# A written order for every instruction, eleven matmuls on a constant tile, and a band drained by head halves

## The chip, the cores and the metric

The kernel runs on one core of a Trainium2 chip. The metric is the device time in microseconds of one execution; the median of the runs shown is compared. The engines are TensorE (PE; PEld are its weight loads), VectorE (DVE), ScalarE (ACT), GpSimd (POOL) and SyncE (SP). POOL and SP only start DMAs here, apart from one mask that POOL makes.

## The reference

Inputs: x of 8 batches x 4224 tokens x 192 channels, a convolution weight of 8 heads x 7 taps, and three matrices w_q, w_k (192 x 64) and w_out (192 x 192), all float32.

```
w   = softmax(weight, over the 7 taps)
y   = causal convolution of x along the tokens: each head of 24 channels with its 7 taps
W   = (y @ w_q) @ (y @ w_k).T / 8          (4224 x 4224 for each batch)
out = relu(W @ y) @ w_out
```

## The kernel before

The 4224 x 4224 matrix is never built: W @ y is (y @ w_q) @ M with M = w_k.T (y.T y) / 8, so a batch needs its Gram matrix y.T y (192 x 192) once. All matrix work is in bfloat16.

*Opening.* `load_w` (SP) brings the taps. POOL makes the identity `ident`; VectorE spreads it to `step`, and TensorE transposes that (`turned`), which ScalarE copies out (`stept`). VectorE also makes `by_tap`, `other` and `own` from the identity, and then the softmax as a chain `mx`, `sub`, `mine`, `ex` (ScalarE), `sm`, `rc`, `wn`, `taps`. From `taps` and `stept` TensorE builds the convolution's band matrix (8 heads, 128 x 128 each): two `fill` products `spread` it to PSUM, half of the columns of all heads in each, and two `band` copies (L527) drain them to the tile BAND, one on ScalarE, one on VectorE. Zeroing of half a dozen tiles lies on VectorE in between.

*A batch.* Tokens are cut into 35 chunks of 122. x is loaded by POOL's queue and cast on the way, in groups of chunks (four groups in batch 0, of 9, 9, 9 and 8 chunks; two in the others). For every group and every pair of heads (`hp` 0 to 3) `gen_conv` multiplies BAND with the chunks; the result is evacuated to `y` (L671). Then follow transposes of y (`tr_lo` L395 and L396, `tr_hi` L726) with evacuations `ytl` and `yth`; the product with w_q (`wq`, L751 and L755) in five token blocks of at most 1024; the Gram matrix (`gram`, L787, six products of up to 6 chunks), its copy (`g`), a transpose (`turn`, `gt`), and the mixing matrix M (`m`, line 829 on) with its copies `ms`. After that, for each token block, `mix_lo` (L878) and `mix_hi` (L890), relu evacuations `rt` and `rh` (L907 ScalarE, L908 VectorE), `fin_hi` (L935) and `fin_lo` with w_out, output copies `out` (L970) and stores by SP (L978). Most products are two halves of 64 columns next to each other in the array ("128x64", recorded at L391 and L392 where the helper `halves` makes them); `mix_lo` and `fin_hi` use halves of 64 rows ("64x128").

*Weights.* SP loads w_q, w_k, w_out (`load_q`, `load_k`, `load_o`, three DMAs each) once the second group of x has landed. ScalarE casts them (L596): three casts `casts_q` that `wq` needs, five `casts_k` that `m` needs, two `casts_o` that `fin_hi` and `fin_lo` need.

*Order.* All work is a list of operations (`Op`), 987 in before. An operation names what it `needs` (waited for by semaphores), what it comes `after` (order alone) and what PSUM banks it takes; seven banks go round, bank 7 holds the Gram matrix. `Planner.plan` walks through time with estimated lengths and gives each operation a place, an engine (evacuations may run on ScalarE or VectorE) and a bank, always the ready operation with the lowest number from the table TURNS. `Program.place` then sets the waits. Each engine runs its own list in that order.

Of the kernel before, what the change touches and what calls it, by code (L numbers as in the profile page):

```python
# [1 line left out]

# [10 lines left out]
TURNS = [  # L13
    int(t) / 1000
    for t in """
-9360 -9860 -8870 -8880 -9260 -9760 -9760 -9160 -9060 -8960 -8910 -8910 -8860 -9360 -9310 -9360 -9360
-9300 -9290 -9280 -8360 -8260 -8210 -8360 -8160 -7960 -7910 -7860 -7360 -7260 -6960 -7260 -4360 -10360
-4260 -4160 -4060 -4040 -3360 -3260 -3160 -4360 -4360 -4360 -4360 -4360 -4360 -4360 -4360 -4360 -4360
-3360 -3340 -3260 -3240 -2360 -2340 -2260 -2240 -1360 -1340 -1260 -1240 -360 -340 -260 -240 640 660 740
760 1640 1660 1740 1760 2640 2660 2740 2760 -480 -5256 -3269 -5639 -2436 -6119 -4785 -6922 -2697 -6547  # L20
-2900 -8184 -3709 -11773 -2741 -3270 -6090 -11945 -3405 -6849 535 -5290 -3070 -5355 -2914 -5199 -4248
-3270 -5203 -8176 -5200 -3617 1049 7270 -1527 1452 -125 437 -1115 2575 669 4462 -4008 2241 -736 2188
-3392 2688 -366 4671 2314 4774 1510 -5859 -1080 1650 3655 -2805 -2225 2863 3712 -4982 -214 3624 -440
5811 168 -43 -4182 2328 1099 2977 4333 5544 2125 -4960 -5487 -5264 -3044 -1246 -5292 -632 -6217 -764
-74 -1078 1645 -1059 -604 310 -1847 1633 809 1261 1148 1774 613 1995 -221 2133 3240 -1868 3227 -220 725
-412 3895 1345 -3908 -437 2412 1145 -3912 1759 7529 -2401 -2511 -376 -45 -770 179 75 1157 1606 377 1178
2478 1419 2696 -2691 660 4785 4565 7183 -1945 323 1366 4118 -874 -955 202 -527 -342 -901 930 -907 356
2535 1985 1382 772 4127 1260 -1111 124 1160 1068 -949 2843 737 1947 1165 1141 1963 1865 1015 1391 1447
1702 -74 1049 2157 -573 -696 2171 3091 -3875 1621 1815 2057 1336 1560 3406 350 3930 1811 1631 806 1533
-2176 120 -160 307 697 392 -607 2158 1443 1095 4683 784 2578 2771 4703 2742 7357 3260 5899 3463 6217  # L30
3645 8560 -333 6048 2165 -3227 -299 4804 1442 -269 2464 1033 2330 -2282 2380 4417 716 -49 3007 5023
2635 1331 4441 4948 2995 6849 3538 5333 2785 2768 -3179 -2909 4430 6167 8185 2441 2170 3478 2909 2541
554 -2341 2444 1927 -821 1930 2471 1683 3865 3015 2812 1681 1913 2901 2236 -1040 2160 2775 2437 2022
2264 1982 2456 530 2945 -625 83 2391 2437 -247 4869 10274 3843 686 -2295 3278 468 -2877 2621 3234 3552
5619 5142 2314 3447 -712 2811 2566 3158 2537 2842 2785 -1373 2551 2194 3151 4852 2972 5013 3067 6779
3044 1235 3763 8267 3776 5123 4769 7025 4778 6514 4876 4862 2843 3189 4464 -186 3400 3287 1517 170 3082
4632 173 2822 4141 2345 4919 -1156 3870 4328 3579 2730 2456 3119 1411 4084 5177 4842 -327 4148 4784
2483 12403 11388 12726 1688 187 6372 10131 3246 4258 -1702 3458 4182 -118 2930 2729 1882 4669 8253 3861
3544 1615 3872 -172 2986 3160 3716 -1740 4531 9062 4005 3598 4951 3990 4363 2435 3391 -188 774 5121
6256 1049 3585 3961 4077 3890 4171 3621 2923 4666 7097 2748 2343 3820 2734 3811 2033 5780 3818 8021  # L40
2648 2954 4015 5571 3280 -1286 3326 1296 4205 -77 4486 1455 4875 3311 5075 4171 5445 4695 5467 3840
5547 6065 4545 4764 3889 874 4988 5384 3296 1407 5065 3706 4229 1167 4799 5495 -1008 2735 5015 4824
-216 1086 4797 3220 6247 4075 6903 8096 2585 2446 2397 3366 12419 11466 9645 4504 4002 2353 3004 4592
2447 1923 4855 3304 3544 3930 4268 4563 -31 1642 3776 4290 -862 3100 4826 6478 4160 4860 2445 3040 6705
3413 4148 6792 4180 4104 2785 4391 4686 4414 786 5937 2381 5714 4010 4678 4791 3602 4621 5486 -3702
4694 4691 4776 4745 8565 4811 2733 1579 4439 3726 3846 1552 3006 3416 5091 3731 3114 391 4950 -191 4947
1241 5561 6938 5922 7844 6076 5816 6857 5549 6431 8495 5919 4361 1180 965 5336 3713 5074 2853 2377 5685
3499 1703 6336 5580 6743 3976 5914 890 3735 -850 6119 5447 4947 4119 5702 6592 2952 2914 3851 5062
11027 10134 10283 4336 4832 2354 5585 5204 5235 5902 4279 5332 6811 4930 5452 70 7184 7777 5311 5310
3592 2752 3699 4914 5160 5093 886 6992 7265 5826 4610 2412 5386 6402 2677 5391 5863 3510 6078 4797 3048  # L50
3549 7308 4286 5112 2810 5621 5940 3872 3652 3847 6176 6516 2312 5811 4551 3444 5310 2800 3910 6703
2902 3118 6150 4601 5838 5604 6069 7926 5802 5058 6795 5408 6694 6497 7055 7466 7544 6117 8040 8562
2857 4878 6430 1709 6339 6247 4084 2149 3587 4651 7375 5911 5923 8233 4224 5104 7135 8548 7626 1422
6752 7520 5954 8811 9981 10001 3331 2861 1100 5523 5736 7942 8989 6855 6991 3418 3771 5267 6754 6792
5257 8583 2774 5930 5621 6098 8589 5981 7588 10163 5667 7262 8790 2009 6160 6573 7890 9275 9286 4367
8366 1994 4430 8376 2928 6391 6798 7671 9079 8471 6945 8447 929 3104 8245 1738 6621 7113 7765 8298
10610 7609 8976 2499 6811 5339 3124 4383 3701 4861 7650 5674 5118 6955 3022 7026 1967 7057 1554 7391
6867 7378 5794 8478 7540 10493 11198 10567 7886 9868 8667 7608 6132 7813 12143 8053 10500 4734 5726
10278 10809 6108 7660 6892 9279 8811 10480 9400 11789 6610 6051 11636 12987 12320 10573 10429 10064
11172 6766 7180 6653 8881 8940 8302 8163 3734 5115 8337 5917 10881 1732 6196 10991 548 6570 3947 6628  # L60
5684 11786 5374 8456 5972 5205 7358 2365 6800 7531 8553 12143 9541 7507 4239 2615 6653 8229 3661 7031
8556 8852 7269 9218 4711 5758 2449 5650 7927 7690 7261 10545 9140 8476 10487 4525 3241 2208 7451 8457
7788 6544 11624 6678 6638 3216 7890 3616 6282 3822 7930 5698 8782 6900 4062 5129 6641 6131 8120 8832
8094 4423 8160 8786 8210 8027 5877 5536 6062 1738 8351 8563 8713 4799 8391 5602 10941 9278 9705 9844
6685 7724 8581 9175 4769 3738 8621 7276 9572 10940 8347 11120 8993 5619 8811
""".split()
]

COL2, ROW2 = "128x64", "64x128"


class Op:


    n = 0

    def __init__(self, engines, emit, ns, needs=(), after=(), banks=0, drains=None, vt=0.0, mode=COL2, tail=0.0):
# [21 lines left out]
        self.size = 0  # L99
        Op.n += 1  # L100
        self.id = Op.n


class Planner:

    LAT = {"PE": 240.0, "ACT": 145.0, "DVE": 140.0, "POOL": 150.0, "SP": 0.0}
    SWITCH = 145.0

    STAY = 0.865

    HOLD = 1

    def __init__(self, nbank, first_bank):
# [164 lines left out]
def bass_lightweight_conv__then__hypermixer_token_mlp_kernel(  # L280
# [93 lines left out]
    def bank(i, n=1):  # L374
        return PS[:, i * 512 : (i + n) * 512]
# [683 lines left out]
```

## Time and profile before

| | us |
|---|---|
| median of 3 runs | 177.33 (177.2 to 178.14) |
| span of the profiled execution, first to last instruction | 175.7 |
| TensorE busy | 157.1 (89% of the span) |
| VectorE, ScalarE, GpSimd busy | 118.0, 123.5, 30.3 |
| all DMA | 40.36 MB, mean 230 GB/s |

The profile is one execution; beside its span it has no time of its own, so the span is held against the median of the runs. Busy shares are averages over stages, and a busy TensorE is not TensorE at its peak: the lengths of its matmuls overlap, so the step from one start to the next is the better measure. "issue" after an idle time means that nothing the profile shows was waited for. A line such as L391 is that of a helper, and stands for several products.

### The profile page before, as it was taken

Reading aid. Unit: us, or ns where it says so; the run is one execution under the profiler, and the core shown is the slowest. Engines: PE = TensorE matmul, PEld = TensorE weight load, DVE = VectorE, ACT = ScalarE, POOL = GpSimd, SP = SyncE. Lnnn points to the kernel's source line nnn. Section 1 sums busy time; section 2 is a strip of 40 time slices with the busy share of each in tenths; the row PEclk is TensorE's granted clock in tenths of the full one; section 3 lists DMA queues with packets and bytes.
Section 4 is the critical chain, followed back from the end, with each engine's and each line's share of the span. In section 5 each row is a group of like instructions: output and inputs, shape, how many; then the busy total and the mean of one; then the engine's idle time right before and its main releaser. Section 6 shows DMA issues by size and latency. Waiting matters only on the chain.

```text
span 175.7 us, 7099 instructions
## 1 busy us (share of the span) xinstructions
PE 157.1 (89%) x3226; PEld 121.7 (69%) x3226; DVE 118.0 (67%) x216; ACT 123.5 (70%) x206; POOL 30.3 (17%) x39
## 2 busy tenths in 40 slices
PE   0289799888999999899989979999999999999990
PEld 0179666776787787668778766878767777877550
DVE  6556587765766677586787738689688675765740
ACT  3243677597787948668648747888888896698980
POOL 7999452524230000000000000000000000000000
PEclk9999999999999999999999999999999999999995
DMA  3999999999999999999999999067283045987787
GB/s 30 162 189 186 205 191 193 191 196 277 193 279 194 286 309 268 343 250 243 304 264 282 237 194 348 24 244 297 103 343 127 4 175 216 356 347 309 265 303 262
DMA packets 48157, 40.36 MB, mean 230 GB/s; under 512 B 37632, under 2 KB 40960, under 8 KB 48128
## 3 DMA queue, kind: packets, MB, share of 16 engines
q0 software_dynamic: 36128, 13.61, 65.1%
q1 hardware_dynamic: 12000, 26.31, 40.9%
q8 instruction: 25, 0.41, 0.9%
q14 instruction: 4, 0.03, 0.1%
HBM read 27.56 MB, written 25.95 MB: 305 GB/s over the span
## 4 chain that ended last, share of the span: by engine, by line
PE 88%; issue 4%; DVE 3%; ACT 2%
PE ps L391 25%; PE ps L787 14%; PE ps L935 8%; PE ps L392 7%; PE ps L395 6%; PE ps L726 6%; PE ps L878 5%; PE ps L751 4%; PE ps L890 4%; PE ps L755 4%; PE ps L396 3%; ACT rt L907 1%; ACT out_sb L970 1%; DVE band L527 0%; DVE xw L416 0%
## 5 line engine op out<-in xcount | busy, mean ns | idle before, releaser
L970 ACT COPY out_sb<-ps 128x768 f32<-128x768 f32 (+1 forms) x46 | 34.7, 768 | 15.1 <-PE ps L392 11.3
L671 ACT CAST y<-ps 122x816 bf16<-122x816 f32 (+3 forms) x46 | 35.7, 791 | 13.2 <-PE ps L392 12.8
L907 ACT ACTIVATE rt<-ps 128x1024 bf16<-128x1024 f32 (+3 forms) x44 | 34.1, 800 | 6.4 <-PE ps L878 4.5
L787 PE MATMUL ps<-y 122*64 122x192 bf16 (+4 forms) x840 | 33.8, 222 | 2.2 <-issue 2.2
L970 DVE COPY out_sb<-ps 128x768 f32<-128x768 f32 (+1 forms) x26 | 21.6, 840 | 19.7 <-PE ps L392 18.5
L392 PE MATMUL ps<-wol,rt 128*64 128x192 bf16 x264 | 33.9, 255 | 1.0 <-issue 1.0
L787 PEld LDWEIGHTS ps<-y 122*64 122x64 bf16 (+1 forms) x840 | 31.1, 112 | 4.9 <-issue 2.8
L565 POOL DMA_DIRECT2D xw<-in_x_dram x34 | 29.9, 893 | 22.3 <-issue 21.5
L391 PE MATMUL ps<-wol,rt 128*64 128x192 bf16 x264 | 33.7, 255 | 0.0
L391 PE MATMUL ps<-xw,band 128*64 128x432 bf16 (+3 forms) x144 | 31.8, 335 | 1.5 <-DVE band L527 0.9
L392 PE MATMUL ps<-xw,band 128*64 128x432 bf16 (+3 forms) x144 | 32.1, 337 | 1.1 <-issue 1.1
L391 PEld LDWEIGHTS ps<-wol,rt 128*64 128x64 bf16 x264 | 24.1, 138 | 8.1 <-issue 2.0
L908 DVE TENSOR_SCALAR rt<-ps 128x512 bf16<-128x512 f32 (+3 forms) x36 | 23.6, 674 | 8.2 <-PE ps L878 7.6
L671 DVE CAST y<-ps 122x864 bf16<-122x864 f32 (+3 forms) x26 | 23.6, 912 | 8.0 <-PE ps L392 7.5
L698 DVE COPY ytl<-ps 128x976 bf16<-128x976 bf16 (+1 forms) x40 | 23.0, 591 | 3.9 <-PE ps L396 3.3
L392 PEld LDWEIGHTS ps<-wol,rt 128*64 128x64 bf16 x264 | 24.1, 138 | 1.2 <-issue 1.2
L396 PE MATMUL ps<-ident,y 122*64 122x122 bf16 x280 | 21.1, 219 | 0.0
L395 PE MATMUL ps<-ident,y 122*64 122x122 bf16 x280 | 21.0, 219 | 0.0
L935 PE MATMUL ps<-woh,rt 64*128 64x192 bf16 x264 | 20.4, 250 | 0.2 <-ACT rt L907 0.2
L395 PEld LDWEIGHTS ps<-ident,y 122*64 122x64 bf16 x280 | 18.1, 112 | 2.0 <-issue 0.5
L726 PE MATMUL ps<-ident,y 122*64 122x122 bf16 (+1 forms) x344 | 17.1, 220 | 1.3 <-DVE y L671 0.7
L396 PEld LDWEIGHTS ps<-ident,y 122*64 122x64 bf16 x280 | 17.7, 112 | 0.0
(95 smaller groups left out, 218.8 us busy)
## 6 DMA issues: line engine op xcount, KB each, us to landing
out_dram<-out_sb SPq DMA_DIRECT2D x28, 768.0 KB, 5.1
xw<-in_x_dram POOLq DMA_DIRECT2D x7, 816.0 KB, 33.2
xw<-in_x_dram POOLq DMA_DIRECT2D x7, 768.0 KB, 33.7
out_dram<-out_sb SPq DMA_DIRECT2D x8, 384.0 KB, 3.3
xw<-in_x_dram POOLq DMA_DIRECT2D x2, 432.0 KB, 8.3
out_dram<-out_sb SPq DMA_DIRECT2D x8, 96.0 KB, 4.3
xw<-in_x_dram POOLq DMA_DIRECT2D x1, 384.0 KB, 5.2
xw<-in_x_dram POOLq DMA_DIRECT2D x8, 45.8 KB, 25.0
```

The lines of the kernel that those rows point to most:

```text
L391: e.matmul(out[0:64], lhsT[:, 0:64], rhs, **k)
L392: return e.matmul(out[64:128], lhsT[:, 64:128], rhs, **k)
L395: e.transpose(out[0:64], in_[:, 0:64], identity)
L396: return e.transpose(out[64:128], in_[:, 64:128], identity)
L565: lambda e, op, part=part: e.dma_start(*part),
L671: return e.copy(dst, src) if op.engine == "ACT" else e.tensor_copy(dst, src)
L726: last = e.transpose(ps[64 * i : 64 * i + HI, o : o + w], Y[0:w, yb, c, LO:D], IDENT[0:w, 0:w])
L787: mm = e.matmul(bank(GB)[p : p + 64, o : o + z - r], Y[0:w, yb, c, r : r + 64], Y[0:w, yb, c, r:z], start=st, stop=end, skip_group_check=True,
L907: return e.activation(dst, src(), AF.Relu)
L908: return e.tensor_scalar(dst, src(), 0.0, None, op0=ALU.max)
L935: last = e.matmul(bank(op.bank + a)[:, o : o + D], RT[64 * a : 64 * a + HI, slot, 2, i:n:nt], WOH[64 * a : 64 * a + HI, :], start=i == q, ...
L970: return e.copy(dst, src) if op.engine == "ACT" else e.tensor_copy(dst, src)
```

## The change

The table TURNS and the planner's search go. In their place stands PLAN, a list of 993 turns, each an operation's number, its engine (P TensorE, A ScalarE, D VectorE, G POOL, S SP) and, for a product, its PSUM bank. `plan` now reads that list. Numbers count the operations as they are added. Those that the prediction speaks of: 0 load_w, 1 the new memset, 15 step, 16, 18 and 37 the three run-ups, 17 turned, 20 by_tap, 22 own, 23 mx, 30 taps, 31 and 34 the fills, 32, 33, 35 and 36 the bands, 38 to 43 the loads of batch 0, 44, 45 and 46 load_q, load_k and load_o, 47 to 49 casts_q, 50 to 54 casts_k, 55 and 56 casts_o, 110 and 112 evacuations y of the last group of batch 0, 143 tr_hi, 151 and 152 grams, 145, 129 and 133 wq, 154 turn, 166 and 160 the first convolutions of batch 1, 881 the last batch's m. POOL's turns are in the same order as before; SP's are not (load_k now stands ahead of load_q, and some stores change places).

Three new TensorE operations multiply a tile RUNUP of zeros with itself, 128 columns by 512, into bank 7: four matmuls ahead of `turned`, six between it and the fills, one between the fills and the first convolution.

The band: a fill now makes all columns of four heads (16 pairs of halves in all, of 64 columns, where there were 8 of 128), and each fill is drained by two copies of two heads, the first fill's on ScalarE, the second's on VectorE. A convolution of a head pair needs only the copy that brings its two heads.

```diff
-TURNS = [
-    int(t) / 1000
-    for t in """
--9360 -9860 -8870 -8880 -9260 -9760 -9760 -9160 -9060 -8960 -8910 -8910 -8860 -9360 -9310 -9360 -9360
...
+PLAN = """
+39G 2D 14G 1D 38G 8D 40G 41G 9D 42G 43G 57G 58G 59G 60G 61G 62G 63G 7D 64G 20D 22D 65G 66G 67G 68G 69G 70G
+12D 15D 71G 72G 73G 5D 74G 75G 76G 77G 78G 79G 0S 80G 81G 23D 16P 17P4 19A 24D 21D 25D 3D 26A 6D 27D 28D 29D
+30D 45S 18P 31P0 33A 32A 34P3 10D 35D 36D 37P 4D 87P5 88D 91P3 89P0 92A 11D 44S 90A 85P2 86D 147P 127P6
+117P3 118D 97P4 98A 93P2 94A 95P1 128D 99P0 100A 107P5 103P4 104D 96A 119P3 13D 105P1 46S 106D 101P0 102D
+149P 109P2 108D 148P 115P1 116A 54A 111P4 120D 135P6 113P0 114D 121P3 110A 112A 150P 131P2 152P 151P 143P4
+125P0 123P1 122D 136D 52A 49A 51A 139P5 153D 47A 50A 48A 126D 144D 145P4 129P6 154P3 132D 133P2 124D 130A
+146A 140D 53A 166P0 155D 167A 160P5 156P4 159A 157A 158A 134D 161D 162P2 164P0 137P4 141P5 220P6 163D 165A
+190P0 178P1 191D 179D 138A 176P2 242P4 177D 186P0 222A 82G 206P 56A 142A 187D 168P5 169A 174P1 244D 207P
...
+921D 891A 874P 806S 900P3 907P5 909A 903P0 904P 862P2 901P 902A 895S 863D 905D 930P6 932A 876P 877P 875P
+878D 929P4 918P2 914P5 911P0 931A 879P4 880D 912P 915P 920A 916A 881P4 906S 882A 913D 884A 917S 864P2 858P3
+859D 925P0 883A 922P5 933P4 865D 923P 924A 938P3 926P 934P 866P2 927A 928S 937P5 940D 870P3 935D 867A 871A
+962P4 964A 961P0 963A 939D 949P2 951D 941P5 942P 950P4 945P0 946P 973P2 936S 943A 944S 947A 948S 952D 957P4
+958P 969P0 970P 959A 960S 975D 953P4 954P 955D 974P3 971A 972S 985P2 987D 965P0 966P 967D 986P6 956S 976A
+981P4 982P 983D 977P2 978P 979D 968S 988A 989P0 984S 980S 990P 991A 992S
 """.split()
...
-COL2, ROW2 = "128x64", "64x128"
+COL2, ROW2, FULL = "128x64", "64x128", "128x128"
...
     def plan(self):
+        drains = {}
         for op in self.ops:
+            if op.drains is not None:
+                drains.setdefault(op.drains.number, []).append(op)
+        users = [[] for _ in range(self.nbank)]
+        place = {}
+        for turn in PLAN:
+            number, engine, bank = re.fullmatch(r"(\d+)([PADGS])(\d*)", turn).groups()
+            op = self.ops[int(number)]
+            op.engine = self.ENGINES[engine]
+            assert op.engine in op.engines and op.number not in place
             if op.banks:
+                op.bank = int(bank)
+                for i in range(op.bank, op.bank + op.banks):
+                    op.needs += users[i]
+                    users[i] = drains[op.number]
+            assert all(x.number in place for x in op.needs + op.after)
+            place[op.number] = len(self.order)
             self.order.append(op)
         assert len(self.order) == len(self.ops)
...
+    RUNUP = sbuf("runup", [128, 512], BF16)
...
+    def run_up(n, needs=(), after=()):
+
+        def emit(e, op):
+            last = None
+            for _ in range(n):
+                last = e.matmul(bank(GB)[:, 0:512], RUNUP[:, 0:128], RUNUP[:, :], start=True, stop=True)
+            return last
+
+        return add("PE", emit, 213.5 * n, needs=needs, after=after, mode=FULL, kind="run_up")
+
+    zero_r = add("DVE", lambda e, op: e.memset(RUNUP[:, :], 0.0), 200)
     one = add("DVE", lambda e, op: e.memset(IDENT[:, :], 1.0), 100, vt=-9.5)
...
     turned = add(
         "PE",
         lambda e, op: turn_halves(e, bank(op.bank).bitcast(BF16)[:, 0:128], STEP[:, :], IDENT[:, :]),
-        60, needs=[step, ident], banks=1, vt=-9)
+        60, needs=[step, ident], after=[run_up(4, needs=[zero_r])], banks=1, vt=-9)
+    run_2 = run_up(6, after=[turned])
     stept = add(
...
     bands = []
-    for q0, engine in ((0, "ACT"), (4, "DVE")):
-
-        def spread(e, op, q0=q0):
+    fills = []
+    for half in range(2):
+
+        def spread(e, op, half=half):
             last = None
-            for q in range(q0, q0 + 4):
+            for q in range(8):
                 last = halves(
                     e,
-                    bank(op.bank)[:, (q - q0) * 128 : (q - q0 + 1) * 128],
+                    bank(op.bank)[:, 64 * q : 64 * q + 64].rearrange("p (i h) -> p i h", h=4),
                     STEPT[0:112, 112 - 16 * q : 240 - 16 * q],
-                    TAPS[0:112, :, :].rearrange("p i h -> p (i h)"),
-                    start=q == q0,
-                    stop=q == q0 + 3,
+                    TAPS[0:112, :, 4 * half : 4 * half + 4],
+                    start=q == 0,
+                    stop=q == 7,
                     skip_group_check=True,
                 )
             return last
 
-        fill = add("PE", spread, 260, needs=[taps, stept], banks=1, vt=-7 + 0.1 * q0)
-
-        def band(e, op, q0=q0, fill=fill):
-            dst = BAND[:, :, 16 * q0 : 16 * q0 + 64]
-            src = bank(fill.bank).rearrange("p (j h) -> p h j", h=H)
-            return e.copy(dst, src) if op.engine == "ACT" else e.tensor_copy(dst, src)
-
-        bands.append(add(engine, band, 550, drains=fill, vt=-6.9))
+        fill = add("PE", spread, 215, needs=[taps, stept], after=[run_2, *fills], banks=1)
+        fills.append(fill)
+        for pair in range(2):
+
+            def band(e, op, h0=4 * half + 2 * pair, k=2 * pair, fill=fill):
+                dst = BAND[:, h0 : h0 + 2, :]
+                src = bank(fill.bank).rearrange("p (j h) -> p h j", h=4)[:, k : k + 2, :]
+                return e.copy(dst, src) if op.engine == "ACT" else e.tensor_copy(dst, src)
+
+            bands.append(add("ACT" if half == 0 else "DVE", band, 300, drains=fill))
+    run_3 = run_up(1, after=fills)
...
-                "PE", conv, mm_ns(n * GRP, 2), needs=[*load[b, gi], *bands, zero_x, zero_x0], after=ev_needs, banks=nb, vt=vt, kind="conv")
+                "PE", conv, mm_ns(n * GRP, 2), needs=[*load[b, gi], bands[hp], zero_x, zero_x0], after=[*ev_needs, run_3], banks=nb, vt=vt, kind="conv")
```

## The prediction

> **What bounds the kernel now.** I read the page first, then the table of waits cut to TensorE, then the timeline of the first 24 us, engine by engine, and last the table of stretches for the tail.
>
> ```profile
> PE   157.1 (89%) x3226; PEld 121.7 (69%) x3226; DVE 118.0 (67%) x216; ACT 123.5 (70%) x206; POOL 30.3 (17%) x39
> ...
> PE 88%; issue 4%; DVE 3%; ACT 2%
> ...
> q8 instruction: 25, 0.41, 0.9%
> ```
>
> TensorE holds 88% of the chain that ended last; the 4% "issue" come back below. The next lines are all of its waits (total, times, longest):
>
> ```profile
> PE ps L395 <- DVE step L435: 3.6, 1, 3.6
> PE ps L391 <- DVE taps L494: 2.9, 1, 2.9
> PE ps L787 <- issue: 2.2, 2, 1.3
> PE ps L392 <- issue: 2.1, 2, 1.1
> PE ps L391 <- DVE band L527: 0.9, 1, 0.9
> PE ps L726 <- DVE y L671: 0.7, 1, 0.7
> PE ps L391 <- issue: 0.6, 1, 0.6
> PE ps L726 <- issue: 0.5, 1, 0.5
> ```
>
> 8.1 us (3.6+2.9+0.9+0.7) are waits before 11.2 us; 5.4 us are "issue"; between 11.2 and 163 us TensorE waits for no other engine. So time is won either in the opening or in those issue waits. The opening, from the timeline (start, length, idle before in brackets):
>
> ```profile
> 6.82 0.31 PE L391 MATMUL ps<-taps,stept 112*64 112x128 bf16 x1 [2.91 <-DVE taps L494]
> ...
> 7.93 0.69 DVE L527 CAST band<-ps 128x512 bf16<-128x512 f32 x1 [1.16 <-PE ps L392]
> ...
> 8.76 0.36 PE L391 MATMUL ps<-xw,band 128*64 128x216 bf16 x1 [0.88 <-DVE band L527]
> ...
> 9.10 0.38 PE L391 MATMUL ps<-xw,band 128*64 128x216 bf16 x1
> ...
> 9.28 0.38 PE L391 MATMUL ps<-xw,band 128*64 128x216 bf16 x1
> ...
> 15.76 0.25 PE L391 MATMUL ps<-xw,band 128*64 128x216 bf16 x1
> ...
> 15.85 0.25 PE L391 MATMUL ps<-xw,band 128*64 128x216 bf16 x1
> ...
> 20.09 0.30 ACT L596 CAST wkl<-wlo 128x128 bf16<-128x128 f32 x1 [0.87 <-DMA whi<-in_moe_w_k_dram]
> ...
> 20.48 0.54 PE L787 MATMUL ps<-y 122*64 122x192 bf16 x12 [1.28 <-issue]
> ```
>
> The same 216-column pair comes every 0.18 us at 9.1 and every 0.09 at 15.8: TensorE runs at half rate until about 15 us, though the page's clock row shows 9 from the start. What the full rate would save after 8.76 is half of what ran there, some 5.2 us of work, so 2.6 us at most.
>
> **The change, part by part.**
>
> *Constant tile.* One memset of 256 words on VectorE (120 words took 0.16, so about 0.3) and eleven 128x512 matmuls. No row shows that form; at 512 columns the 64-column halves of the wq product step by 0.21 us at full rate, so I take 0.21 full, 0.43 half. Four run from 1.45 us to 3.15, the turned step follows at 3.85 (VectorE now does by_tap and own ahead of it; before 3.60), then six until 6.6 at half rate. They lie under the 3.6 and 2.9 us of waiting. If that cover were gone they would cost 11 x 0.43 = 4.7 us. What do they do to the clock? In before the step changed after some 3.8 us of unbroken work (11.11 to 15); a stretch with 0.7 us missing in the middle (8.76 to 11.7) did not change it. The new work has one hole of 0.7 us, at 3.15. I take the full rate from about 7 us.
>
> The Trainium skill ("TensorE: Matmul & The Clock Gate", Part 1) says the array idles at half clock and is released after a busy window of about 3.4 us that runs free of the kernel's start. The rows agree with the two rates; by the rule the release comes between 4.9 and 8.3 us if a window may hold the hole, and as late as 10.5 us if it may not (estimates). In that last case the sum below would be 175.6 for 175.1.
>
> *Taps and band.* Five memsets and the eps write leave the stretch ahead of the taps, so these end about 0.5 us earlier (6.76 to 6.2); the spread starts at 6.3 to 6.6, since it stands behind the six matmuls. The spread has 32 matmuls of 64 columns for 16 of 128: the same columns. The drain is four casts of 256 columns for two of 512 (0.58 ACT, 0.69 DVE). 256 are not shown; between 192 (0.32 to 0.36) and 432 (0.52, 0.65) I take 0.40 and 0.45. First convolution at about 7.5, the second at 8.2 behind the second VectorE cast; before, 8.76.
>
> *To the second batch.* The loads set floors, and POOL's queue keeps its order: landings (issue plus time to landing in the DMA view) at 6.5, 10.8, 13.1, 15.1 us for the four groups of batch 0, 21.3 for the first of batch 1. So the first group's lead dies: the gram waits for its four evacuations (two casts of 0.65 on VectorE behind the bands: about 10.2), the second group's x lands at 10.8. At full rate the chunks then go by 12.1, 13.2 (load), 15.2 (load). Next is ScalarE: in the new order cast 54A (a wk weight) stands ahead of y evacuations 110A and 112A, and wk is now fetched first. Its DMAs, issued from 10.8, land about 16.9 as wq's do now (11.78 + 5.1). So 54A runs at 17.0 and the two y casts end at 18.2; grams 152P and 151P and three transposes bring TensorE to 20.3. The wq product 145P then needs casts 49A, 47A and 48A, and wq is now second: its last piece lands between 18.9 and 20.1, as wk's does now (13.55 + 5.1 to the wait that ends at 20.09), plus five casts at 0.25: 20.15 or 21.35. First convolution of batch 1: 21.4 or 22.6, where before starts it at 23.53 (and had done 0.17 us less). Gain 2.3 or 1.1. I take 2.0, nearer the first, because the landing at 20.1 is one late DMA engine, the others are at 18.8. The floor of 21.3 forbids more.
>
> *Issue waits.* 25 packets of 0.41 MB are 16 KB each; 6452 TensorE instructions over 25 are 258 per packet. The six issue waits (from 19.20, 32.64, 39.08, 70.06, 89.60 and 102.10) stand at 442, 949, 1203, 2474, 3239 and 3748 TensorE instructions in the table of stretches: 2, 1, 5, 3 and 2 times some 254 apart. All lie while x is loading (to 106 us), none after. I read them as instruction pages that come late behind the loads. Eleven matmuls with their weight loads (22) and the finer spread (32) add 54 instructions. At 12 us the first new boundary comes; the next at 18.0, six us on, so the 1.28 of before is probably gone within the gain above. Of the remaining 4.05 us: with the mean step of each kind of matmul in the trace, the shortest pages under load last 5.2 to 5.6 us in the old order (four below 5.6) and 5.6 upward in the new. I take 3.0: gain 1.0. Bounds: 3.0 gained, 1.5 lost.
>
> The Trainium skill ("Runtime: NRT & Kernel Launch", Instruction fetch mechanics) calls a page crossing mostly hidden. The trace disagrees with 5.4 us of waits; by that rule the term would be nothing and the sum 176.1.
>
> *The written order.* Only 132 of 483 TensorE ops keep their place relative to each other, and 124 evacuations change engine. The ops themselves are the same. Pairs with 64 rows alternate with the others 113 times instead of 107; a step from fin_hi to fin_lo takes 0.172 us, inside a kind 0.080, so +0.55. Other crossings get cheaper, and with the mean step of each crossing both orders sum to 42.6 us. Between 0 and 0.55 I take +0.3. Waits on evacuations: none before from 11.2 to 163 us; the new order has as many TensorE ops less than 0.8 us of TensorE work behind the product that feeds them (20, was 18), but more that reuse a bank within 1.1 us (89, was 50). I take +0.5, between 0 and a wait per batch of the size of the issue waits (0.5 to 1.3, so 7 x 0.8 = 5.6). Stores keep SP to themselves and shift by a place or two.
>
> *Tail.* After the last mixing matrix (157.1 us) ScalarE has 12.9 us of evacuations (19; 0.80 per 768-column output, 1.02 per 1024-column relu) and VectorE 8.8;
>
> ```profile
> 157.40:171.30 13.90, 13.24 (x208) 8.29 (x201) 8.55 (x16) 12.63 (x20) 0.00 (x0) 1.00 0.80 297
> ```
>
> in that stretch ScalarE, the fifth figure, is busy 12.63 of 13.90. The new split is 9.2 and 11.6 (0.96 and 1.22 on VectorE). The longer side drops 1.3, but four fewer TensorE ops (38 for 42) are left behind that product, by their mean steps 1.4 us, so it comes that much later. Net 0; bounds 1 either way.
>
> **Sum.** −2.0 +0.3 −1.0 +0.5 +0 = −2.2 us. The profiled execution: span 175.7 to 173.5. No view gives its time beyond the span; the median 177.33 lies 1.6 above, which is kept: 175.1.
>
> **The rivals.**
> - *The clock is not released early* (zeros do not count, or the hole at 3.15 spoils it). For: a 0.7 us hole did spoil it at 10.4. Against: the new hole lies before, not inside, the work from 3.85 on. The opening is then about 1.0 slower, since loads and weights set floors anyway: 176.1.
> - *The weights take the place of the cold clock.* 54A ahead of two y casts, wq fetched second: were both landings a further 1 to 1.5 us late, as single DMA engines are here (the last of 16 landing marks 0.70 us behind the others for the second x load, 1.24 for wk), the opening gives nothing: 177.1, no difference.
> - *Slower: TensorE meets waits in every batch.* Banks are reused sooner; one wait of 0.8 in each of seven batches makes 5.6 against 2.7 of gains: 180.2. It decides from (2.7+0.9)/7 = 0.5 us per batch. Against: before shows not one such wait in 150 us with a bank slack little longer.
>
> **How the numbers follow.** Forecast 0.60 (own range 173.2 to 176.4), cold clock 0.13, weights 0.12, waits 0.15. A measurement of this kernel tells about 0.5% (0.9 us: 176.4 to 178.2 is no difference). Faster: 0.57 + 0.11 + 0.02 = 0.70; same 0.14; slower 0.16. The range 173.0 to 177.6 takes in the first three cases, the lower end from the issue waits all gone, and leaves out the waits.
>
> **What would show it.** Pairs of 216 columns 0.09 apart at the first convolution; the first convolution of batch 1 (432 columns) at 21.4 to 22.6; issue waits of about 3 us in all; no TensorE wait on ACT or DVE between 24 and 160 us; the last mixing matrix some 1 us earlier than 157.1 and a tail of the same length. Wrong would be waits on ps evacuations in the middle, or a gram behind 112A after 19 us.

## The result, and the profile after

The changed kernel takes 181.84 us (median of 4 runs, 181.19 to 182.1) where the kernel before, on the same chip, takes 177.29 (177.2 to 178.14). The ratio is 1.0248, 95% interval 1.0224 to 1.0273: 2.5% slower, where 175.1 us was forecast. The profiled execution (the fastest of its four, 181.19) has a span of 179.5 us for 175.7.

From the page of the kernel after: busy times, the shares of the chain that ended last, and the clock row.

```profile
PE 163.1 (91%) x3253; PEld 121.3 (68%) x3253; DVE 127.2 (71%) x224; ACT 117.3 (65%) x201; POOL 30.3 (17%) x39
...
PEclk9999999999699999999999999999999999999996
...
PE 75%; DMA 9%; DVE 6%; ACT 5%; issue 2%; DVEq 0%; SPq 0%; ACTq 0%
```

TensorE held 88% of the chain in before and holds 75% here; DMA, which was not in that line, has 9%. "issue" fell from 4% to 2%. The clock row has a 6 in its eleventh slice, at 45 to 49 us. The waits of TensorE (total, times, longest) name the place:

```profile
PE ps L315 <- ACT out_sb L906: 2.3, 1, 2.3
PE ps L311 <- DVE out_sb L906: 2.0, 1, 2.0
PE ps L334 <- DVE runup L339: 1.4, 1, 1.4
PE ps L311 <- DVE y L607: 1.3, 1, 1.3
PE ps L315 <- DVE wmx L393: 1.0, 1, 1.0
...
PE ps L312 <- issue: 0.7, 2, 0.4
```

Two are waits of TensorE on copies into `out_sb`, which before does not have at all. L906 is the copy of a result from PSUM into an output slot. What the copies themselves wait for is in the timeline (start, length, idle before with its releaser), ScalarE and SP in one stretch, then the other wait:

```profile
36.98 2.44 ACT L906 COPY out_sb<-ps 128x768 f32<-128x768 f32 x3 [0.58 <-PE ps L312]
...
45.05 0.32 ACT L906 COPY out_sb<-ps 128x192 f32<-128x192 f32 x1 [3.13 <-DMA out_dram<-out_sb]
...
45.42 0.24 PE L315 MATMUL ps<-ident,y 122*64 122x122 bf16 x1 [2.26 <-ACT out_sb L906]
...
69.93 1.82 DVE L906 COPY out_sb<-ps 128x768 f32<-128x768 f32 x2 [2.30 <-DMA out_dram<-out_sb]
...
70.94 0.24 PE L311 MATMUL ps<-gsb,wkl 128*64 128x128 bf16 x1 [1.96 <-DVE out_sb L906]
```

and the two stores in the chain that ended last (start, length):

```profile
37.81 7.16 DMA out_dram<-out_sb
...
60.20 9.63 DMA out_dram<-out_sb
```

This is the mechanism. There are four output slots (`NOUT = 4`), so a copy of output job n waits until the store of job n-4 has landed. The store issued at 37.81 lands 7.16 us later; ScalarE was ready for the next copy into that slot at 41.92 (45.05 less 3.13 of idle), 4.1 us behind the issue. ScalarE stands still for 3.13 us, the bank that it should empty stays full, and TensorE stands still for 2.26. At 60.20 it happens again: 9.63 us to land, VectorE ready after 7.4. That store was issued 0.42 us behind another of 768 KB (59.78), which landed in 7.5.

A late store is only half of it, for before has such a wait too:

```profile
65.83 0.80 ACT L970 COPY out_sb<-ps 128x768 f32<-128x768 f32 x1 [2.43 <-DMA out_dram<-out_sb]
```

ScalarE was free 6.5 us behind the issue of that store (56.91), which took 8.8 us to land, and TensorE did not stop. The product that this copy drains ended at 64.57, so the store alone held it for 1.2 us (to 65.75), and five other products (two `fin_lo`, a `wq`, two `gram`) kept TensorE at work to 66.68, when the next product took the bank. In after the product ended at 42.35, the store held its copy for 2.6 us (to 44.97), and only four short products (two `tr_hi`, a `turn`, a `mix_hi`) stood between, to 43.16. So a copy that waits for its store costs TensorE only what the products up to the next use of the bank don't cover.

The landing time was in the trace of before, in the DMA view (operation, count, KB each, median us from issue to landing), here for its stretch from 35 to 46 us and then from 106 to 140:

```profile
out_dram<-out_sb SPq DMA_DIRECT2D x1, 768.0 KB, 7.2
...
out_dram<-out_sb SPq DMA_DIRECT2D x7, 768.0 KB, 4.5
```

A store of 768 KB takes 7.2 us there beside the x loads (medians of 8.1, 7.3 and 7.6 in the stretches 46 to 60, 60 to 75 and 75 to 106) and 4.5 when they are done. The least room that before left in that time, from a store's issue until the engine is free for the next copy into its slot, is the 6.5 us above; the written order left 4.1.

Of the marks that the prediction named, these came as forecast: the 216-column pairs 0.09 us apart (9.54, 9.63, 9.72) in the first convolution; the first convolution of batch 1 at 21.82 (forecast 21.4 or 22.6; before 23.53). These did not: issue waits of 2.0 us in all (the 1.3 of L311 above, explained below, and the 0.7) for "about 3"; the spread of the band at 7.50 for 6.3 to 6.6; the last mixing matrix at 161.7 for some 156; and the two waits in the middle.

### The profile page after: what moved, and what is told of

Its sections match the earlier page's. It is cut to its first block, busy times and chain, and to the rows that moved or that the text cites. A ratio compares the mean times of both kernels' runs of the same rounds, so it can differ in the third digit from the quotient of the medians.

```text
span 179.5 us, 7144 instructions
## 1 busy us (share of the span) xinstructions
PE 163.1 (91%) x3253; PEld 121.3 (68%) x3253; DVE 127.2 (71%) x224; ACT 117.3 (65%) x201; POOL 30.3 (17%) x39
## 4 chain that ended last, share of the span: by engine, by line
PE 75%; DMA 9%; DVE 6%; ACT 5%; issue 2%; DVEq 0%; SPq 0%; ACTq 0%
PE ps L311 20%; PE ps L723 13%; DMA out_dram<-out_sb 9%; PE ps L871 7%; PE ps L315 6%; PE ps L312 6%; PE ps L814 5%; PE ps L662 4%; PE ps L687 4%; PE ps L826 4%; PE ps L691 3%; PE ps L316 2%; ACT out_sb L906 2%; DVE y L607 1%; DVE out_sb L906 1%
## 5 line engine op out<-in xcount | busy, mean ns | idle before, releaser
L906 ACT COPY out_sb<-ps 128x768 f32<-128x768 f32 (+1 forms) x42 | 31.5, 766 | 19.5 <-PE ps L312 13.9
L607 ACT CAST y<-ps 122x816 bf16<-122x816 f32 (+3 forms) x45 | 34.2, 790 | 12.2 <-PE ps L312 11.4
L843 ACT ACTIVATE rt<-ps 128x1024 bf16<-128x1024 f32 (+3 forms) x45 | 31.7, 740 | 8.8 <-PE ps L814 5.1
L906 DVE COPY out_sb<-ps 128x768 f32<-128x768 f32 (+1 forms) x30 | 25.3, 856 | 14.5 <-PE ps L312 12.0
L723 PE MATMUL ps<-y 122*64 122x64 bf16 (+3 forms) x840 | 32.8, 220 | 1.0 <-DVE y L607 0.9
L311 PE MATMUL ps<-wol,rt 128*64 128x192 bf16 x264 | 33.6, 257 | 0.0
L312 PE MATMUL ps<-xw,band 128*64 128x432 bf16 (+3 forms) x144 | 30.7, 323 | 0.4 <-issue 0.4
L311 PE MATMUL ps<-xw,band 128*64 128x432 bf16 (+3 forms) x144 | 30.8, 322 | 0.0
L607 DVE CAST y<-ps 122x864 bf16<-122x864 f32 (+3 forms) x27 | 24.6, 921 | 8.1 <-PE ps L312 7.7
L844 DVE TENSOR_SCALAR rt<-ps 128x512 bf16<-128x512 f32 (+3 forms) x35 | 26.1, 762 | 5.6 <-PE ps L826 4.2
L311 PEld LDWEIGHTS ps<-wol,rt 128*64 128x64 bf16 x264 | 24.2, 139 | 6.9 <-issue 1.5
L315 PE MATMUL ps<-ident,y 122*64 122x122 bf16 x280 | 21.6, 219 | 3.2 <-ACT out_sb L906 2.3
L316 PE MATMUL ps<-ident,y 122*64 122x122 bf16 x280 | 21.6, 220 | 0.0
L871 PEld LDWEIGHTS ps<-woh,rt 64*128 64x128 bf16 x264 | 11.3, 114 | 9.0 <-issue 2.2
```

Of the source, the lines that this page charges most:

```text
L311: e.matmul(out[0:64], lhsT[:, 0:64], rhs, **k)
L312: return e.matmul(out[64:128], lhsT[:, 64:128], rhs, **k)
L315: e.transpose(out[0:64], in_[:, 0:64], identity)
L316: return e.transpose(out[64:128], in_[:, 64:128], identity)
L607: return e.copy(dst, src) if op.engine == "ACT" else e.tensor_copy(dst, src)
L723: mm = e.matmul(bank(GB)[p : p + 64, o : o + z - r], Y[0:w, yb, c, r : r + 64], Y[0:w, yb, c, r:z], start=st, stop=end, skip_group_check=True,
```

## The experiments

Edits are against the changed kernel unless another is named; of the long lines of PLAN and of some calls only the part that changes is shown.

To compare kernels along their course, I take the moment at which the kernel before has a given amount of TensorE work behind it (each product's matmuls by the mean step of their kind, the constant tile not counted) and ask how much later or earlier another kernel has the same amount. Negative is ahead of before, in us. Each row is one profiled execution, so some tenths between two rows tell nothing:

| at (us of before) | 24 | 43.5 | 46 | 55 | 75 | 120 | 169 |
|---|---|---|---|---|---|---|---|
| after | -1.95 | -1.30 | +1.75 | +2.82 | +4.40 | +2.88 | +3.64 |
| e1 six slots | -1.46 | -1.34 | -1.24 | -1.24 | -1.80 | -2.93 | -2.18 |
| e3 no constant tile | -0.11 | +0.20 | +2.56 | +2.55 | +4.82 | +3.27 | +4.19 |
| e4 table early | -2.39 | -1.62 | +2.38 | +2.46 | +5.63 | +3.70 | +4.44 |
| e6 kept busy | -1.97 | -1.61 | +1.25 | +1.24 | +3.49 | +3.01 | +3.76 |
| e7 six slots, table early | -2.80 | -2.92 | -2.82 | -2.82 | -3.39 | -4.25 | -3.50 |
| e10 = e7, no tile | -1.12 | -0.83 | +0.60 | +0.60 | +2.10 | +0.91 | +1.84 |
| e12 = e7, narrow tile | -1.03 | -1.01 | -0.91 | -0.91 | -1.47 | -2.06 | -1.32 |
| e2 before's order, opening | -2.37 | -2.83 | -2.17 | -2.18 | -1.48 | -1.98 | -1.75 |
| e9 before's order, band | -0.92 | -2.61 | -2.55 | -1.91 | -2.15 | -2.01 | -2.02 |
| e11 before's order, tile | -0.88 | -1.54 | -1.53 | -0.93 | -1.23 | -0.69 | -0.70 |

### e1: six output slots

```diff
-    NOUT = 4
+    NOUT = 6
-    RUNUP = sbuf("runup", [128, 512], BF16)
+    RUNUP = YTL[:, 0:512]
```

> The changed kernel with six output slots in place of four (the constant tile lies in the first 512 columns of ytl to make room). Theory S (store slots): the loss comes from output copies that wait until the store of the same slot has landed (2.26 us of TensorE wait at 43.2, 1.96 at 69.0) and from the half clock that follows the first (46.6 to 50.0). Then both waits and the half clock go: 181.8 - 2.3 - 2.0 - 1.2 to 1.7 = about 176, range 175.3 to 177.5. Rival O (the written order is slower everywhere, by bank reuse and kinds of crossing): the waits move elsewhere and less than 1 us is won, 180.8 or more.

175.27 us (174.61 to 175.55), ratio 0.9875 (0.9845 to 0.9905): 1.25% faster than before. The waits of TensorE are now

```profile
PE ps L334 <- DVE ytl L339: 1.4, 1, 1.4
PE ps L315 <- DVE wmx L393: 1.0, 1, 1.0
PE ps L723 <- DVE y L607: 0.9, 1, 0.9
PE ps L311 <- issue: 0.9, 1, 0.9
PE ps L315 <- ACT y L607: 0.8, 1, 0.8
PE ps L312 <- issue: 0.7, 2, 0.4
```

without any line for `out_sb`. With nothing but the slots changed (and the constant tile moved into `ytl` to make room) the course stays at -1.2 to -2.9 to the end, so the output slots are the whole of the loss: 6.6 us between the medians.

### e8: five output slots

```diff
-    NOUT = 4
+    NOUT = 5
```

> The changed kernel with five output slots. By the written order the closest copy into a slot then stands 2.5 us of TensorE work behind the store that must have landed (0.85 with four slots, 4.5 with six), and a store takes 7 to 8.5 us while x loads. Theory S: a wait remains, smaller or fewer of them: 176.3 to 179.5, between the 181.6 of four slots and the 175.3 of six. If it is not the store that counts but the room in bank and engine: no step between four and six that goes with the distance, 181 or more.

176.66 us (176.36 to 178.24), ratio 0.9946 (0.9916 to 0.9977). One wait is left, 1.7 us for a ScalarE copy that starts at 65.9 us, 10.0 us behind the issue of the store five jobs before (55.9). Four slots, five and six give 181.84, 176.66 and 175.27: the cost follows the reuse distance.

### e2: before's order with the new opening

PLAN holds the order, engines and banks of before, with the constant tile (16P, 18P, 37P) and the four band copies (33A 32A, 36D 35D) put in:

```diff
-39G 2D 14G 1D 38G 8D 40G 41G 9D 42G 43G 57G 58G 59G 60G 61G 62G 63G 7D 64G 20D 22D 65G 66G 67G 68G 69G 70G
...
+0S 2D 1D 39G 6D 7D 5D 8D 14G 9D 10D 38G 11D 12D 15D 20D 16P 17P0 18P 22D 21D 40G 4D 19A 3D 13D 23D 24D 41G
+25D 26A 42G 27D 28D 29D 43G 30D 31P1 34P2 37P 57G 33A 32A 36D 35D 58G 91P3 87P4 89P5 92A 85P6 88D 59G 90A
...
```

> The order of before for all that it had, with the constant tile and the band by head halves alone. Theory S: the opening is worth 1.0 to 2.0 us, and the middle and the tail stay as before: 175.3 to 176.3, no TensorE wait on an output copy. Rival L (landings of x and of the weights eat the opening): 177 to 177.6. Rival C (the constant tile itself costs, since more TensorE instructions bring later pages): over 177.8.

175.68 us (175.3 to 176.27), ratio 0.9906 (0.9876 to 0.9937). The opening is no part of the loss; the new order on four slots is. How this order spends its gain is taken up with e9 and e11.

### e3: the written order without the constant tile

```diff
     def run_up(n, needs=(), after=()):
+        return None
-16P 17P4 19A
+16P4 17A
...
```

> The changed kernel without the eleven matmuls on the constant tile (its memset stays). If the tile gives the full clock from 9 us: half rate until about 14, the first convolution of batch 1 some 1.0 to 1.5 later than 21.8; how much of it lasts depends on the store waits, which hang on when stores start: 181.8 to 183.3. Rival: the tile does nothing for the clock or the landings hide it: 181.0 to 181.8, since the fills need not wait for the six matmuls.

182.99 us (182.15 to 184.3), ratio 1.034 (1.028 to 1.040): 1.2 us slower than after. Full rate begins at 15.3 us and the course is 1.5 us behind after's at 43.5 (+0.20 for -1.30). The waits on `out_sb` shrink (1.94, 0.63, 0.48 for 2.26, 1.96), since TensorE comes later to the same stores. The edit also takes 22 instructions out of TensorE's stream, and the issue waits are 3.1 us here for 2.0, so the 1.2 us is not the price of the clock alone (see e10 and e12).

### e4: the table load ahead

The trace of ScalarE in after has its table load where before does not:

```profile
4.69 1.28 ACT L377 ACT_TABLE_LOAD   x1 [4.69 <-PE ps L316]
5.98 0.18 ACT L377 COPY stept<-ps 128x24 bf16<-128x24 bf16 x1
6.06 0.30 ACT L414 ACTIVATE wex<-wex 128x112 f32<-128x112 f32 x1
```

In before it runs at 0.80 and the copy behind it at 3.95. The copy of `stept` needs two things: `turned` from TensorE and `zero_s`, the memset of its tile (5D). In before that memset stands ahead of `step`; the written order puts it behind `step` (15D), from which `turned` is made, so the wait on VectorE is no longer implied by the one on TensorE. The copy then has two waits to make, and the one on TensorE is made at the table load ahead of it. The experiment moves one token:

```diff
-12D 15D 71G 72G 73G 5D 74G
+12D 5D 15D 71G 72G 73G 74G
```

> The changed kernel with the memset of stept put ahead of step on VectorE, so that the load of ScalarE's table (1.28 us) no longer stands behind the wait for the turned step (4.69 in the changed kernel, 0.80 before). Taps end about 1 us earlier than 7.44, but the fills stand behind the six constant matmuls that end at 7.2: first convolution 0.3 to 0.4 earlier. If that lasts: 181.4; if loads and stores eat it: 181.8; if the table load costs its whole 1.2: 180.6.

```profile
0.81 1.28 ACT L377 ACT_TABLE_LOAD   x1 [0.81 <-PEq L980]
4.64 0.18 ACT L377 COPY stept<-ps 128x24 bf16<-128x24 bf16 x1 [2.55 <-PE ps L316]
4.87 0.30 ACT L414 ACTIVATE wex<-wex 128x112 f32<-128x112 f32 x1
```

The exponential is 1.2 us earlier (4.87 for 6.06). The time is 181.39 us (180.9 to 181.92), ratio 1.0226 (1.0192 to 1.026), not distinguishable from after: the course is 0.3 us ahead of after's at 43.5, and the same two stores, with waits of 2.33 and 2.00 us, take it back. In this execution the second wait too is followed by half clock, from 72.43 to 75.84 us.

### e5: before's order, new opening, six slots

On top of e2:

```diff
-    NOUT = 4
+    NOUT = 6
```

> The order of before, with the constant tile, the band by head halves and six output slots: against the run with the written order and six slots it shows what the written order is worth once no output copy waits for a store. The planner of before kept at least 6.9 us of TensorE work between a store and the next copy into its slot while x loads, so the slots should win nothing here: 175.4 to 176.0, as with four slots. If the written order is better by its fewer page waits (2.0 us for 5.4), it stays 0.4 or more above the written order with six slots (175.3); if the crossings of the written order cost that again, both are equal.

176.0 us (175.72 to 176.5), ratio 0.9899 (0.9866 to 0.9931), against 175.68 for e2. In before's order slots buy nothing. The order of after without its store waits (e1) is 0.7 us below that by the medians and 0.4 by the ratios, with intervals that overlap: the two orders are not told apart here.

### e6: TensorE kept busy ahead of the two waits

The table of stretches shows what the first wait does to the clock (TensorE's busy time is the second figure; the granted clock stands behind the five engines):

```profile
43.14:46.55 3.41, 1.15 (x26) 0.72 (x26) 0.93 (x3) 1.50 (x3) 0.66 (x1) 1.00 1.44 236
67.03:70.44 3.41, 1.96 (x42) 1.54 (x42) 1.11 (x3) 1.13 (x2) 0.00 (x0) 1.00 1.14 342
...
46.55:49.96 3.41, 3.41 (x44) 2.66 (x43) 1.70 (x4) 2.06 (x3) 0.64 (x1) 0.50 1.55 212
```

After 3.41 us in which TensorE worked for 1.15, the next 3.41 run at half clock; 1.96 us of work were enough to keep it. The experiment puts sixteen constant matmuls of 256 columns before each of the two waits:

```diff
+    keep_on(16)
+    keep_on(16)
-287P0
+993P 287P0
-326P4
+994P 326P4
```

> The changed kernel with sixteen more matmuls on the constant tile (256 columns into the unused part of bank 7, 1.7 us) ahead of each of the two products that wait for an output copy (43.2 and 69.0). The waits stay, TensorE is kept at work in them. If the half clock after the wait costs what it looks like (3.4 us at half rate, 1.2 to 1.7): no half clock between 45 and 50, and 179.8 to 180.5 for 181.4 to 181.8. If the stores hold everything up anyway: 181.4 or more.

182.19 us (181.84 to 183.23), ratio 1.0253 (1.021 to 1.0296). The clock is unbroken, and at 55 us of before the course is 1.6 us better than after's (+1.24 for +2.82), where it was 0.3 better at 43.5 us, ahead of the waits: about 1.3 us is what filling the first wait and keeping the clock won there. At the end nothing is left (+3.76 for +3.64); TensorE waits 1.27 us at 107.4 for a ScalarE copy into an output slot, which it does not in after. The half clock is a consequence of the first wait. That what it costs is made up at the later stores, where whoever comes earlier waits longer, is how I read these figures; no run shows it alone.

### e7: six slots, table early, six and four constant matmuls

```diff
-    NOUT = 4
+    NOUT = 6
-12D 15D 71G 72G 73G 5D 74G
+12D 5D 15D 71G 72G 73G 74G
-after=[run_up(4, needs=[zero_r])]
+after=[run_up(6, needs=[zero_r])]
-    run_2 = run_up(6, after=[turned])
+    run_2 = run_up(4, after=[turned])
```

> Six output slots, ScalarE's table early, and the constant matmuls as six, four and one instead of four, six and one, so that the hole at 3.3 us is filled and the fills come about 1 us earlier. First convolution at about 8.0 for 9.0; the landings of x (10.4, 12.7, 14.9) and of the weights take a part of it back: 174.3 to 175.0 against 175.3 with six slots alone. If the landings take it all: 175.3.

174.38 us (173.75 to 174.53), ratio 0.9797 (0.9765 to 0.983): the fastest version here, 2% faster than before. The token that gained nothing in e4 and the new split of the constant matmuls, which no run tries alone, are together worth 1.6 us at 43.5 (-2.92 for e1's -1.34), and TensorE waits for x itself:

```profile
PE ps L311 <- issue: 0.9, 2, 0.6
PE ps L312 <- issue: 0.7, 2, 0.4
PE ps L311 <- DMA xw<-in_x_dram: 0.6, 2, 0.3
```

### e9 and e11: each half of the opening alone, in before's order

e9, on top of e2:

```diff
     def run_up(n, needs=(), after=()):
+        return None
-16P 17P0 18P
+16P0
...
```

> The order of before with the band by head halves, without the matmuls on the constant tile (its memset stays). Against the run of both (175.7) it shows what the tile is worth in an order without store waits. If the clock is the larger part: half rate until about 15, the band brings the first convolution some 0.3 earlier, 176.9 to 177.3. If the band is the larger part: 175.7 to 176.3.

e11, on top of e2, with the fills and band copies of before:

```diff
-            for q in range(8):
+            for q in range(q0, q0 + 4):
...
-                    TAPS[0:112, :, 4 * half : 4 * half + 4],
+                    TAPS[0:112, :, :].rearrange("p i h -> p (i h)"),
...
-                dst = BAND[:, h0 : h0 + 2, :]
+            dst = BAND[:, :, 16 * q0 : 16 * q0 + 64]
```

> The order of before with the constant tile alone; band spread and drained as in before (two casts of 512). Theory A, the constant tile is worth nothing in this order and the gain of the opening (175.4 to 175.7) came with the band halves: full rate from about 9 us, but 177.0 to 177.8. Rival B, either part alone shifts the instruction pages and brings the gain through fewer issue waits: 175.3 to 176.3, issue waits below 3.5 us in all where before has 5.4. Rival C, the full rate is itself worth 1 to 2 us here and the two parts overlap: 175.5 to 176.3 with issue waits of 5 us or more.

The band halves alone: 175.42 us (175.27 to 176.2), ratio 0.9894 (0.9833 to 0.9955). The constant tile alone: 175.86 (175.02 to 176.6), ratio 0.9892 (0.9861 to 0.9923). Both together were 175.68. The theories for e11 are not told apart: its time is that of B and C, its issue waits (4.5 us) lie between theirs, and the span of its profiled execution is only 1.0 us under that of before (174.7) where the medians differ by 2.0; that execution is the longest of its eight (176.6). Each alone gives the whole gain, so they don't add, and neither gives it where it works: at 18.9 us of before e9 and e11 are 0.6 us behind, at 24 about 0.9 ahead, since before loses 1.28 us to an issue wait in between. The issue waits of e9:

```profile
PE ps L724 <- issue: 1.1, 2, 0.6
PE ps L872 <- issue: 0.9, 1, 0.9
PE ps L688 <- issue: 0.6, 1, 0.6
PE ps L663 <- issue: 0.2, 1, 0.2
```

2.8 us for 5.4 in before; e11 has 4.5, e2 4.5. In e2 the early full rate is followed by issue waits of 1.05 us at 16.3 and 1.32 at 22.5, where e9 at half rate until 16.4 has none. These kernels differ from before by 32 (finer spread), 22 (constant tile) and 54 TensorE instructions ahead of everything else. That raised a question that the next two answer: is the tile worth its clock, or its instruction count?

### e10 and e12: e7 without the tile, and with a narrow one

e10, on top of e7:

```diff
     def run_up(n, needs=(), after=()):
+        return None
```

> The written order with six output slots and the table load moved ahead (the last version, 174.38 us beside 177.91), without the eleven constant matmuls. Theory A, the constant tile is worth what it was worth with four slots (182.99 without, 181.84 with): full rate only from about 15 us, first convolutions at half rate, the lag behind before at 40 us about 1.0 to 1.5 us worse than -2.9, time 175.4 to 176.0. Rival B, it is worth nothing, as in the order of before (175.68 with, 175.42 without), because full rate only reaches the x loads and the instruction pages sooner: 174.2 to 174.8, waits on x loads gone and issue waits no more.

e12, on top of e7:

```diff
-                last = e.matmul(bank(GB)[:, 0:512], RUNUP[:, 0:128], RUNUP[:, :], start=True, stop=True)
+                last = e.matmul(bank(GB)[:, 0:16], RUNUP[:, 0:128], RUNUP[:, 0:16], start=True, stop=True)
```

> The version with six slots and the early table load (174.38 us beside 177.91), with its eleven constant matmuls kept in place and in number but 16 columns wide for 512, so that the count of TensorE instructions ahead of every later one is as with the constant tile and the array is idle as without. Theory A, instruction pages: without the eleven matmuls (179.77 us) every page boundary fell 22 TensorE instructions later in the work, and the issue waits were 4.9 us for 1.6. Here they are again below 2.5 us in all, at the same instruction counts as with 512 columns, and what stays is the half rate until about 15 us: a lag of 1.0 to 2.1 us against the 512-column version at 40 us that does not grow behind it, time 175.4 to 176.8. Rival B, the rate: full rate in the opening alone is worth the 5.4 us, by a chain of later waits: 178.5 to 180, issue waits 4 us or more.

Without the eleven matmuls 179.77 us (178.71 to 180.11), ratio 1.0109 (1.0038 to 1.0181); with eleven of 16 columns 175.85 (175.56 to 176.65), ratio 0.9899 (0.9851 to 0.9948); with eleven of 512 columns 174.38. Neither theory for e10 had the size: 1.6 us above e7 were expected at most, 5.4 came. Theory A for e12 holds. The issue waits of e10,

```profile
PE ps L692 <- issue: 2.0, 2, 1.2
PE ps L312 <- issue: 1.4, 3, 0.7
PE ps L311 <- issue: 1.3, 1, 1.3
PE ps L724 <- issue: 0.2, 1, 0.2
```

and of e12:

```profile
PE ps L312 <- issue: 0.7, 2, 0.4
PE ps L311 <- issue: 0.6, 1, 0.6
PE ps L315 <- issue: 0.2, 1, 0.2
```

e12 has half rate like e10 (216-column pairs 0.18 us apart at 8.5) and is level with it at 24 us of before (-1.03, -1.12). From there it keeps its course, and e10 loses 3.9 us in issue waits at 36.6, 44.3, 58.6 and 65.3 us, where e12 has 0.3 at the first. By the rows shown e10 waits 4.9 us for instructions and e12 1.5. So 22 instructions that compute next to nothing are worth 3.2 us of span (3.9 between the medians) by where they put the later ones, and the full rate in the opening is worth 2.2 (e7 against e12 at 169 us) or, between the medians, 1.5.

That the instructions come in pages fits the positions closely. Over the traces of all fourteen kernels TensorE has 62 waits called issue of 0.15 us or more; counted in recorded TensorE instructions (matmuls and weight loads), each stands 187 to 195 behind a multiple of 254. In e10 the four named stand at 1205, 1459, 1967 and 2221. That a page's fetch was late in each case is still a reading of them.

## Why the prediction was wrong, step by step

**The step that failed** is the last sentence of "The written order": "Stores keep SP to themselves and shift by a place or two." It looked at the queue that issues the stores and left out what a store holds: its slot, until it lands. So it put the waits for stores at nothing. A moved store or copy had to be priced as (landing time) less (time from its issue until an engine is free for the next copy into its slot), and that less what TensorE can still do before it needs the copied bank: 7.2 us less 4.1 at the first place is 3.1, of which TensorE lost 2.26; 9.6 less 7.4 at the second is 2.2, of which it lost 1.96. Landings of 7.2 and 8.1 stood in the DMA view of before. The rest needs the order of output jobs in PLAN and the banks; the same paragraph had gone through the banks, but not through the slots, the other buffers in rotation.

**Waits on evacuations**, +0.5 (0 to 5.6): measured 2.26 + 1.96 and some of the half clock behind the first. The size lies in the range and the place does not. The rival "TensorE meets waits in every batch" had the sign, 180.2 us and the chance of 0.15, but its mechanism, a bank reused sooner, is not enough: e1 has the same banks in the same order, and has no such wait. Nor is a late store enough: before and e2 have ScalarE idle for one (2.43 and 2.39 us), and TensorE goes on. It takes both; no run with four slots and other banks tells their shares apart.

**Opening**, -2.0: -1.95 at 24 us of before, but only by the place of that mark. By then before has its issue wait of 1.28 us behind it (19.20 to 20.48), and after still has its own of 1.27 ahead (22.89 to 24.16). By the same measure after is about 0.5 us ahead at 18.9 us and 0.3 to 0.5 at 25, so the opening by itself gave about half a us; that the sum of 2.0 came out at 24 us is luck. The parts are not right either. Taps ended at 7.4 for the 6.2 forecast, because of the table load; this was to be seen in the place of 5D behind 15D in PLAN, and I had counted only what left the stretch ahead of the taps. What carried it all the same is the clock, full from 9.0 us, inside the widest of the estimates (10.5, which by its own sum, 3.85 and twice 3.4, is 10.7), rather than from 7.

**Issue waits**, -1.0 (3.0 gained to 1.5 lost): behind 24 us of before, after waits 2.0 us (1.27, 0.38 and 0.32) for 4.05, so 2.1 are gained, and 2.5 in e1 (0.87, 0.38 and 0.31), within the bounds. One step of it failed: "the 1.28 of before is probably gone within the gain above". It came back at 22.9 us, as the line `L311 <- DVE y L607: 1.3` shown above. The profile names a cast there that ended 0.2 us earlier, but in e7 the same matmul resumes at 22.54 while that cast runs until 23.02, and there the wait is called issue. In both, and in e1 and e12, it stands behind the same 695 recorded TensorE instructions, and so does a wait of e10, which meets another matmul there. Of the 1.95 at 24 us, 0.65 is gone by 43.5. The Trainium skill ("Runtime: NRT & Kernel Launch", Instruction fetch mechanics) calls such crossings mostly hidden; e10 against e12 has 3.4 us of them, from 22 instructions.

**The written order's crossings**, +0.3, were too small. From 24 to 169 us of before, e1 moves by -0.72, e7 by -0.70 and e12 by -0.29, while their issue waits there are 1.6, 1.6 and 1.5 us for the 4.05 of before, 2.5 less. So the written order itself costs some 1.8 to 2.2 us on the way. The same sum for before's order leaves +0.2 in e9 and -0.3 in e11. In e1 0.8 us of it are gaps of TensorE below 0.15 us, which the list of waits leaves out (0.1 in before); what the rest is, no run shows.

**The tail**, 0: from the last mixing matrix to the end there are 17.8 us in after (from 161.7) and 17.6 in e1 (from 155.9), for 18.5 in before (from 157.2), inside the bounds of 1.

**The cold-clock and weights rivals** fell: full rate came at 9.0, and no wait of TensorE on a cast of a weight is in the list.

With the one missed resource taken out, the number comes out: -2.2 us and 175.1 were forecast, e1 measures -2.18 at the end of its course and 175.27. That is a coincidence of parts. In e1 the opening has -1.5 at 24 us for -2.0, the issue waits -2.5 for -1.0, the written order +1.8 for +0.3, and the waits on evacuations nothing for +0.5. The store slots alone separate the forecast from the result, but the other terms of the sum were off by 0.5 to 1.5 us each and cancel.

## What to carry to other kernels

For every buffer in rotation, banks and output slots alike, hold the distance between release and next use in the new order against the time its release takes under the load of that stage, store landings included. Then count what the engine that would wait can do before it needs the buffer. An order that keeps every operation can still break a distance that the old order had. (The old planner does count a landing, but at 4.0 us for 768 KB when no other store is under way: 1300 + 786432/390 + 700 ns in `Planner.plan`. The 4.1 us would have passed it, so that this count kept the distance is not shown.) And where the instruction stream is long and the DMA queues are full, a change of a few dozen instructions moves every later instruction wait; a small edit's own worth is seen only with the count held fixed, as e12 does.

## What the runs showed of the hardware that was not expected

- Half clock in the middle of a run: in every trace the changes of the clock lie multiples of 3.41 us apart (in after at 9.00, 46.55 and 49.96), and the stretches here are cut on that grid. Two stretches of 3.41 us with 1.15 and (e4) 1.13 us of TensorE work were each followed by 3.41 us at 0.50. A stretch with 1.78 (e4) was too; stretches with 1.96 and 2.88 (after) were not. The last stretch of work in before, 168.69 to 172.11, has 2.15 us and was followed by half clock too, so the busy time alone does not decide. The Trainium skill ("TensorE: Matmul & The Clock Gate", Part 1) has the clock fall after an idle window of about 3.4 us; the length agrees, but here a third to six tenths of the window was work.
- Zeros count as work for the clock: with the constant tile full rate came at 9.0 us (after) and 5.3 (e7), without it at 15.3 (e3) and with matmuls of 16 columns at 15.6 (e12). The same opening gave 9.0, 8.1, 8.7 and 8.5 us in after, e1, e6 and e8.
- Single stores of 768 KB took 7.0 to 11.0 us beside the loads of x (before, after); behind the loads the medians are 4.5 and 4.3.
- ScalarE's table load inherits a wait of the instruction behind it when that one has two: 4.69 us for 0.81, by the place of one memset on VectorE.
- All 62 issue waits of TensorE of 0.15 us or more, in fourteen traces, stand at the same place of a period of 254 recorded TensorE instructions (187 to 195 behind its multiples).
